# Gate products of the first two token groups: GpSimd instead of VectorE, in an attention and gated feed-forward kernel

## The chip, the cores and the metric

The kernel runs on one core of a Trainium2 chip. The metric is the device time of one execution in microseconds (us). The core has five engines that matter here: TensorE (PE, with its weight loads on a line of their own, PEld), VectorE (DVE), ScalarE (ACT), GpSimd (POOL) and SyncE (SP), whose queue issues nearly all transfers.

## The reference

An attention without softmax (two products, k transposed times v and then q times that, followed by a normalisation of each row) gives an array x of 4608 tokens by 512. The feed-forward part is what takes the time:

```
h  = x @ w_in                                    # 4608 x 2048
sp = maximum(h, 0) + log1p(exp(-abs(h)))         # softplus
g  = h * erf(sp)                                 # the gate product
out = g @ w_out                                  # 4608 x 512
```

The third line's multiplication, `h * erf(sp)`, is the operation that the change moves.

## The kernel before

**Groups and units.** Tokens are handled in groups T = 0 to 4 of 512, and the hidden width of 2048 in 16 units f of 128. The first two groups (`FIRST = 2`) run in one loop over n = 0 to 32, with T and f from `divmod(n, FC)`, `FC = 16`. The other three groups run in a second loop, over batches of four units. The change touches only the first loop, roughly 23 us to 241 us of the profile.

**One step n of the first loop.** TensorE computes the hidden unit n (line 940 in group 0; line 589 in group 1, where each operand is cut into a high and a low part and the product is collected in two PSUM tiles, `n_ps` and `m_ps`). ScalarE copies the unit to `h_sb` (lines 953 and 955), and in group 1 VectorE adds the second part, `m_ps`, from PSUM (line 567). ScalarE then computes softplus into `s_sb` (line 971). The function `erf` (line 885) turns `s_sb` into erf in place, for four units at once at the end of each batch of four; in group 1 a batch is split into two calls in neighbouring steps. Then `gates(n)` (line 881) multiplies `hs[n]` by `ss[n]` in place. Five steps after a unit was computed (`LAG = 5`), `project` (line 645) multiplies its gate product with `w_out`. In group 1, all steps share the single pair of PSUM tiles `n_ps` and `m_ps`: the products of step n + 1 into `m_ps` can begin only when VectorE's addition (line 567) of step n has read it.

**Where the gate products stand.** Each step of both groups from n = 4 on issues one, `gates(n - 4)`. In group 1 it stands after the addition of line 567. The products of the last four units, n = 28 to 31 (`whole` is 28), are issued together after the loop:

```
    for n in range(whole, FIRST * FC):
        gates(n)
    low_room.close()
    room.close()
```

After `room.close()`, the memory of the first loop, with the buffers of `h_sb` and `s_sb`, is given to new pools. The first four transfers into one of them, `w_out_parts` (line 834), are issued by SyncE next. The second loop then cuts the tile `h` of the last four units into parts on ScalarE (line 527).

**What else VectorE does in the first loop.** The program order is fixed by hand, and every engine works through its instructions in order. In group 0, VectorE rebuilds weights from loaded words (`w_join`: lines 261, 264, 267 and 274); the word buffers `w_raw` are four in number, and SyncE loads the next one (lines 224 and 229) when line 267 has read the old one. In group 1, VectorE cuts weights into parts (`w_lower`: lines 554 and 557), which line 589 uses a step later and SyncE stores, and it adds line 567. In both, it prepares the attention of the next group (lines 329, 353, 426, 440, 441, 476, 479, 488) and its parts (530 and 533). GpSimd has no work after the first 11 us.

Of the kernel before, what the change touches and what calls it, by code (L numbers as in the profile page):

```python
# [44 lines left out]
ALU = mybir.AluOpType  # L45
# [24 lines left out]
def kernel(  # L70
# [10 lines left out]
    nc = tc.nc  # L81
# [120 lines left out]
    for p in range(NP):  # L202
        nc.gpsimd.dma_start(
            out=q_last[p % 2 * R : p % 2 * R + R, p // 2],
            in_=q[0, 2 * p : 2 * p + 2, G:S, :].rearrange("h r d -> r h d"),
        )
    for i in range(2):
        nc.gpsimd.dma_start(
            out=g_col[i * D : i * D + D, :], in_=g_norm.rearrange("(d one) -> d one", one=1)
# [661 lines left out]
    hs, ss, plain = {}, {}, {}  # L871
# [6 lines left out]
        return i < len(w_order) and w_order[i][0] <= n + ahead  # L878

    def gates(n):  # L880
        nc.vector.tensor_tensor(out=hs[n], in0=hs[n], in1=ss[n], op=ALU.mult)  # L881

    def erf(units):
        for i in units:
# [2 lines left out]
    for n in range(FIRST * FC + 1):  # L887
# [27 lines left out]
        if T == 0 and done >= 0:  # L915
            gates(done)
# [30 lines left out]
        if T < FIRST:  # L947
# [9 lines left out]
            if T == FIRST - 1:  # L957
                if f == 1:
                    x_both = wide.tile([P, KC, G], FP32R, name="x_both", tag="b")
                    for i in range(0, KC, 2):  # L960
                        both_only(x_high[:, i : i + 2], x_low[:, i : i + 2], x_both[:, i : i + 2])
                    x_forms[T] = x_high, x_low, x_both
                gates(done)
                for key in list(w_new):
                    w_lower(*key)
                for key in to_cut[f]:
                    w_upper(*key)
# [26 lines left out]
    for n in range(whole, FIRST * FC):  # L994
        gates(n)
# [9 lines left out]
    def part(h, half):  # L1005
        return h[:, :, half * 2 * P : half * 2 * P + 2 * P]
# [36 lines left out]
    for m in range(first_batch, batches + 1):  # L1043
# [81 lines left out]
        for j in range(J):  # L1125
# [19 lines left out]
            for half in due_halves:  # L1145
                nc.vector.tensor_tensor(  # L1146
                    out=part(h, half), in0=part(h, half), in1=part(s, half), op=ALU.mult
# [38 lines left out]
```

## Time and profile before

| what | value |
| --- | --- |
| median of 3 runs | 907.48 us (907.44 to 908.41) |
| the profiled execution: its own time, and its span | 907.2 us, 905.4 us |
| PE busy, share of the span | 897.1 us, 99% |
| DVE busy | 758.7 us, 84% |
| ACT busy | 593.2 us, 66% |
| POOL busy | 4.7 us, 1%, in 14 instructions |
| gate products of line 881 | 32, 0.68 to 0.69 us each in the middle |

The span runs from the first to the last instruction of the profiled execution; its own time is 1.8 us more. A line such as "L881 DVE TENSOR_TENSOR" names the line of the kernel, the engine and the operation. In a timeline the columns are start, duration, engine, line, operation, output and inputs, and in square brackets the idle time before the instruction and what ended it.

### The profile page before, as it was taken

Reading aid. Unit: us, or ns where it says so; the run is one execution under the profiler, and the core shown is the slowest. Engines: PE = TensorE matmul, PEld = TensorE weight load, DVE = VectorE, ACT = ScalarE, POOL = GpSimd, SP = SyncE. Lnnn points to the kernel's source line nnn. Section 1 sums busy time; section 2 is a strip of 40 time slices with the busy share of each in tenths; the row PEclk is TensorE's granted clock in tenths of the full one; section 3 lists DMA queues with packets and bytes.
Section 4 is the critical chain, followed back from the end, with each engine's and each line's share of the span. In section 5 each row is a group of like instructions: output and inputs, shape, how many; then the busy total and the mean of one; then the engine's idle time right before and its main releaser. Section 6 shows DMA issues by size and latency. Waiting matters only on the chain.

```text
span 905.4 us, 13399 instructions
## 1 busy us (share of the span) xinstructions
PE 897.1 (99%) x4934; PEld 667.6 (74%) x4934; DVE 758.7 (84%) x1093; ACT 593.2 (66%) x784; POOL 4.7 (1%) x14
## 2 busy tenths in 40 slices
PE   8999999999999999999999999999999999999998
PEld 4444446666688888888888888888888888888886
DVE  5799959997788888888888888888888888887677
ACT  5976677775766666665666666666666766665552
POOL 2000000000000000000000000000000000000000
PEclk9999999999999999999999999999999999999999
DMA  9977308999599988988899879988797788778871
GB/s 290 300 225 222 100 30 289 367 343 354 200 377 375 328 297 262 376 306 300 300 328 364 310 238 327 362 303 305 277 346 274 266 311 311 285 285 314 320 265 48
DMA packets 136930, 259.89 MB, mean 287 GB/s; under 512 B 78817, under 2 KB 87265, under 8 KB 136865
## 3 DMA queue, kind: packets, MB, share of 16 engines
q1 hardware_dynamic: 136128, 258.09, 81.3%
q10 hardware_dynamic: 544, 0.82, 0.3%
q8 instruction: 39, 0.64, 0.3%
q14 instruction: 27, 0.21, 0.1%
q0 software_dynamic: 192, 0.13, 0.0%
HBM read 224.40 MB, written 34.60 MB: 286 GB/s over the span
## 4 chain that ended last, share of the span: by engine, by line
PE 94%; DMA 2%; DVE 2%; ACT 1%; issue 0%; SPq 0%; DVEq 0%
PE n_ps L589 48%; PE m_ps L589 24%; PE o_ps L645 10%; PE h_ps L940 5%; PE at_ps L418 2%; PE at_ps L404 2%; DMA w_out_parts<-w_out 1%; DMA w_raw<-in_moe_w_out_dram 1%; PE at_ps L456 1%; PE at_ps L457 1%; PE warm_ps L792 1%; DVE w_e L267 0%; PE o_ps L712 0%; DVE w_in_sb L274 0%; DVE h L881 0%
## 5 line engine op out<-in xcount | busy, mean ns | idle before, releaser
L589 PE MATMUL n_ps<-w_out_parts,g_forms 128*128 128x512 f32 x928 | 230.5, 390 | 0.1
L589 PE MATMUL n_ps<-x_forms,w_in_parts 128*128 128x512 f32 x896 | 224.3, 392 | 0.0
L589 PEld LDWEIGHTS n_ps<-w_out_parts,g_forms 128*128 128x128 f32 x928 | 172.7, 188 | 36.0 <-DMA w_out_parts<-w_out 0.5
L589 PEld LDWEIGHTS n_ps<-x_forms,w_in_parts 128*128 128x128 f32 x896 | 166.6, 188 | 35.6 <-ACT s_sb L885 0.2
L567 DVE TENSOR_TENSOR h<-m_ps,h 128x512 f32<-128x512 f32 x116 | 78.1, 687 | 63.9 <-PE m_ps L589 61.9
L589 PE MATMUL m_ps<-w_out_parts,g_forms 128*128 128x512 f32 (+1 forms) x468 | 124.2, 388 | 0.0
L589 PE MATMUL m_ps<-x_forms,w_in_parts 128*128 128x512 f32 x448 | 119.7, 389 | 0.0
L1092 ACT ACTIVATE h<-n_ps 128x512 f32<-128x512 f32 x112 | 66.2, 594 | 75.0 <-PE n_ps L589 74.7
L1097 ACT ACTIVATE s<-h 128x512 f32<-128x512 f32 x112 | 68.3, 629 | 70.0 <-DVE h L567 70.0
L645 PE MATMUL o_ps<-w_out_sb,h_sb 128*128 128x512 f32 x224 | 101.5, 596 | 0.2 <-DVE h_sb L881 0.2
L589 PEld LDWEIGHTS m_ps<-w_out_parts,g_forms 128*128 128x128 f32 x468 | 87.4, 188 | 18.4
L589 PEld LDWEIGHTS m_ps<-x_forms,w_in_parts 128*128 128x128 f32 x448 | 84.1, 188 | 17.5
L567 DVE TENSOR_TENSOR e<-m_ps,e 128x512 f32<-128x512 f32 (+1 forms) x117 | 80.3, 687 | 15.4 <-PE m_ps L589 5.6
L645 PEld LDWEIGHTS o_ps<-w_out_sb,h_sb 128*128 128x128 f32 x224 | 41.3, 189 | 45.3 <-issue 43.1
L533 DVE SCALAR_TENSOR_TENSOR g_forms<-g_forms 128x1024 fp32r<-128x1024 f32 x58 | 71.1, 1225 | 2.0
L530 DVE TENSOR_TENSOR g_forms<-h,g_forms 128x1024 fp32r<-128x1024 f32 x58 | 70.5, 1216 | 1.1 <-ACT g_forms L527 1.1
L527 ACT ACTIVATE g_forms<-h 128x1024 fp32r<-128x1024 f32 x58 | 58.4, 1049 | 15.3 <-DVE h L1146 7.9
L562 DVE SCALAR_TENSOR_TENSOR e<-n_ps,e 128x512 f32<-128x512 f32 x88 | 60.2, 684 | 7.3 <-PE n_ps L589 7.3
L940 PE MATMUL h_ps<-xT,w_in_sb 128*128 128x512 f32 x144 | 65.1, 595 | 1.1 <-DVE w_in_sb L274 1.1
L1146 DVE TENSOR_TENSOR h<-h,s 128x1024 f32<-128x1024 f32 x56 | 65.9, 1218 | 0.0
L116 ACT ACT_TABLE_LOAD x44 | 56.5, 1283 | 0.8
L940 PEld LDWEIGHTS h_ps<-xT,w_in_sb 128*128 128x128 f32 x144 | 26.9, 190 | 35.4 <-issue 31.4
(138 smaller groups left out, 999.0 us busy)
## 6 DMA issues: line engine op xcount, KB each, us to landing
w_out_parts<-w_out SPq DMA_DIRECT2D x116, 768.0 KB, 6.8
w_in_parts<-w_in SPq DMA_DIRECT2D x112, 768.0 KB, 6.7
w_in<-w_new SPq DMA_DIRECT2D x16, 768.0 KB, 4.6
k_sb<-in_k_dram SPq DMA_DIRECT2D x32, 288.0 KB, 6.3
v_sb<-in_v_dram SPq DMA_DIRECT2D x31, 288.0 KB, 6.3
w_raw<-in_moe_w_in_dram SPq DMA_DIRECT2D x16, 512.0 KB, 5.6
w_raw<-in_moe_w_out_dram SPq DMA_DIRECT2D x8, 1024.0 KB, 5.1
out_dram<-e SPq DMA_DIRECT2D x32, 256.0 KB, 3.5
```

Source lines behind the costliest of these rows:

```text
L116: nc.scalar.preload_act_table_set("softplus")
L527: nc.scalar.activation(high, x, AF.Copy, scale=1.0 + 2.0**-13)
L530: nc.vector.tensor_tensor(out=low, in0=x, in1=high.bitcast(FP32), op=ALU.subtract)
L533: nc.vector.scalar_tensor_tensor(out=both, in0=low.bitcast(FP32), scalar=SHIFT, in1=high.bitcast(FP32), op0=ALU.mult, op1=ALU.add,)
L562: nc.vector.scalar_tensor_tensor(out=out_, in0=ps, scalar=scale, in1=out_, op0=ALU.mult, op1=ALU.add)
L567: nc.vector.tensor_tensor(out=out_, in0=ps, in1=out_, op=ALU.add)
L589: nc.tensor.matmul(ps[:, cols], lhsT=weights(form, k), rhs=moving(form, k)[:, cols], start=(form == forms[0] and k == 0), stop=(form == fo ...
L645: nc.tensor.matmul(o_ps[j], lhsT=g[:, j * P : j * P + P], rhs=w_out_sb[:, f, :], start=(f == 0), stop=last,)
L940: nc.tensor.matmul(plain[i], lhsT=w_in_sb[:, i % FC, c], rhs=xT[T][:, c, :], start=(c == 0), stop=(c == KC - 1),)
L1092: nc.scalar.activation(h[:, i], n_ps, AF.Copy, scale=SHIFT - 1.0)
L1097: nc.scalar.activation(s[:, i], h[:, i], AF.Softplus)
L1146: nc.vector.tensor_tensor(out=part(h, half), in0=part(h, half), in1=part(s, half), op=ALU.mult)
```

## The change

`gates` issues its multiplication on GpSimd. Nothing else in the program is edited: TensorE, ScalarE and SyncE keep their instructions and order, and VectorE's list is the old one without the 32 products. The products of the second loop (line 1146) stay on VectorE.

```
     def gates(n):
-        nc.vector.tensor_tensor(out=hs[n], in0=hs[n], in1=ss[n], op=ALU.mult)
+        nc.gpsimd.tensor_tensor(out=hs[n], in0=hs[n], in1=ss[n], op=ALU.mult)
```

On GpSimd the 32 products stand one behind the other, after the work of the start. The waits of `project` (line 645), of ScalarE's copies into reused `h_sb` buffers (953 and 955), of its cut of line 527 and of SyncE's first `w_out_parts` transfer (834), which were on VectorE's products, are now on GpSimd's.

## The prediction

> **What bounds the kernel now.** I read the page's busy times first, then busy time by stage.
>
> ```profile
> PE 897.1 (99%) x4934; PEld 667.6 (74%) x4934; DVE 758.7 (84%) x1093; ACT 593.2 (66%) x784; POOL 4.7 (1%) x14
> ```
> ```profile
> 60.00:80.00 20.00, 20.00 (x95) 9.43 (x94) 18.74 (x26) 16.77 (x21) 0.00 (x0) 1.00 0.66 199
> 180.00:200.00 20.00, 20.00 (x112) 12.40 (x112) 18.62 (x33) 14.68 (x24) 0.00 (x0) 1.00 0.91 346
> ```
>
> The columns after the stretch are its length, PE, PEld, DVE, ACT, POOL busy (with counts), granted clock and DMA. TensorE is never idle in either stage, at full clock: a relieved VectorE cannot speed it up. VectorE is 93% busy, so there is little room to make it slower. The waits of TensorE between 30 and 270 us say how much there is to win, the same small sum:
>
> ```profile
> PE h_ps L940 <- DVE w_in_sb L274: 0.4, 1, 0.4
> PE o_ps L645 <- DVE h_sb L881: 0.2, 1, 0.2
> ```
> The weight loads add one of 0.5 us, for `w_out_parts`. So the change can gain about 1.1 us at most.
>
> Next, three places where VectorE is near TensorE's path. First, the timelines of ScalarE and VectorE at the first erf batch:
>
> ```profile
> 39.16 2.19 ACT L885 ACTIVATE s_sb<-s_sb 128x512 f32<-128x512 f32 x4
> ...
> 39.70 0.69 DVE L264 TENSOR_SCALAR w_e<-w_e 128x1024 int32<-128x1024 int32 x1
> 40.43 1.23 DVE L267 SCALAR_TENSOR_TENSOR w_e<-w_raw,w_e 128x1024 int32<-128x1024 int32 x1
> 41.80 1.22 DVE L274 CUSTOM_DVE_ANT_0 w_out_sb<-w_e,w_m 128x2048 uint16<-128x2048 uint16 x1
> 42.94 0.68 DVE L881 TENSOR_TENSOR h_sb<-h_sb,s_sb 128x512 f32<-128x512 f32 x1
> 45.47 0.23 DVE L426 COPY x_last<-at_ps 128x64 f32<-128x64 f32 x1 [1.85 <-ACT qT L423]
> ```
> By the chain of waits, line 267's end lets SP issue a `w_raw` load at 41.73; it lands at 46.55, VectorE joins, and TensorE resumes at 50.53, having waited. Line 267 is on the path.
>
> Second, a group 1 step (VectorE, then TensorE):
>
> ```profile
> 182.29 0.69 DVE L554 SCALAR_TENSOR_TENSOR w_new<-w_new,w_in_sb 128x512 fp32r<-128x512 f32 x1
> 183.01 0.69 DVE L557 TENSOR_TENSOR w_new<-w_new 128x512 fp32r<-128x512 f32 x1
> ...
> 184.95 0.68 DVE L567 TENSOR_TENSOR h_sb<-m_ps,h_sb 128x512 f32<-128x512 f32 x1
> ...
> 188.35 1.10 PE L589 MATMUL m_ps<-x_both,w_new 128*128 128x512 f32 x4
> ```
> The addition ends at 185.63 and must end by 188.35, when TensorE writes `m_ps` again: 2.7 us of slack. At 211.82 (next use 215.22) it is 2.7 again, elsewhere 3 to 6 (addition lines against the next `m_ps` lines).
>
> Third, the group's end, in the chain that ended last:
>
> ```profile
> 233.73 0.61 DVE h_sb L881
> ...
> 238.47 1.90 DVE h L881 x3
> ...
> 240.42 0.34 SPq L834
> ...
> 241.76 10.20 DMA w_out_parts<-w_out
> ...
> 252.01 0.73 PE n_ps L589 x2
> ```
> The last four products delay the first `w_out_parts` transfers, and TensorE waits for them at 252.
>
> **What the Trainium skill says.** "GPSIMD Engine Reference", 3.1 Elementwise: a fp32 two-input operation of 2048 elements takes 4497 ns there and 2293 on VectorE, and the input port allows about 2.6 cycles an element at 1.2 GHz. The trace has no such GpSimd instruction; its VectorE side agrees (line 1146 at half the elements: 1218 ns). "SBUF — State Buffer", Who interferes with whom: GpSimd shares a port pair with VectorE; a GpSimd operation that reads SBUF and a VectorE operation with two SBUF inputs, or in a two-port mode, exclude each other, and the later one "**fully blocks**". No run here shows it yet. "VectorE: DVE Perf Modes", The perf-mode tier table: fp32 single-input SBUF operations run at double rate. The trace agrees (0.69 us for line 264 against 1.23 for two-input line 267, both 1024 wide). So 264, 267, 274, 530, 533, 554 and 557 are in conflict; 567, 426, 353 and 678 read PSUM with at most one SBUF input and are not.
>
> **The change part by part.**
>
> Removed from VectorE: 32 x 0.60 us (start to start, 42.94 to the next; 0.68 with the overlapped end) = 19 us. TensorE is full beside it; what this gives is room for what follows.
>
> Price of one product on GpSimd: scaling 4497 by 512/2048 gives 1.12 us as lower bound; a fixed 0.3 us (the upper end that I allow) gives (4497-300)/4 + 300 = 1.35. I take 1.2, an estimate from that page. Alone it is hidden: the products no longer wait in VectorE's queue, so they start when erf ends. The first is ready at 39.8 and `project` wants it at 45.68 by TensorE's line; later ones have more. The extra waits on TensorE, ScalarE and SP replace equal ones on VectorE, so I cost them at nothing, covered by that earliness; with no earliness the first `project` has 2.1 us (43.62 to 45.68). GpSimd's own waits for buffer reuse are for work steps earlier; nothing else queues on it.
>
> (A) First batch, +1.2 us. Product 0 is ready while 264 runs; I take the port to go alternately to whoever waited longest. So product 0 goes in front of 267, which is 1.2 late, as are the `w_raw` load and its join, and TensorE's wait at 50.53 grows from 0.4 to 1.6. 274 becomes 2.4 late and ends at 45.4, just before `project` at 45.68. The 1.85 us idle time then takes the rest. Bounds: 0 (GpSimd loses the port) and 2.4 (two products in front). Later batches of group 0: nothing, since the joins are 6 us or more ahead of use (73.69 against 80.05), and VectorE idles 3.6 us at 119 and 6.3 at 129.
>
> (B) Group 1, +1.8 us. Erf comes in pairs, two pairs in neighbouring steps, so four products fall in some 5 us (erf at 153.8 and 157.0; 181.1 and 184.7; 208.0 and 211.1). Cluster one: four blocks less two removed products are 4.8 - 1.2 = 3.6, against 3.7 (the weight part ends 163.26, line 589 takes it at 166.93) and 4.0 at `m_ps`; nothing. Cluster two: three products run before the addition, 3 x 1.2 - 0.6 = 3.0 against 2.7: +0.3. What is left is 4.8 - 0.6 - 0.3; VectorE's idle times to 208 give back 0.9, four removed products 2.4, so 0.6 remains. Cluster three: 3.6 + 0.6 - 2.7 = +1.5. Bounds: 0 if the port is not contended; if each block also costs VectorE a second 1.2 (a turn lost on either side), A is 2.4 and B (7.2 - 0.6 - 2.7) + (7.2 - 2.7) = 8.4. After 220 VectorE idles 3.5 us twice (lines 567 and 476), and all lateness there ends.
>
> (C) Group end, +0.8 us. The four erfs end 235.71 + 0.63 and then every 0.52 to 237.90. On VectorE the products waited behind a copy (678) and ended 240.36. On GpSimd the first starts at about 236.35, and four end at 236.35 + 4.8 = 241.15. No conflicting VectorE operation runs then. SP's four loads move by 0.8, and TensorE's wait for them grows by that. ScalarE's line 527 moves too; its next on the path, 423 at 244.90, waited 1.5 us anyway, and VectorE's 0.4, 0.2 and 1.3 us idle behind it take the rest. The 0.2 us that `project` gains at 234.38 vanishes in the same wait. Bounds: -0.5 (the whole wait gone) and +1.4 (at 1.35 each).
>
> Sum 1.2 + 1.8 + 0.8 = +3.8 us on 907.2 is 911.0. The median stands 0.3 above that execution: 911.3. Afterwards TensorE is busy to the end, so nothing gives it back.
>
> **The rivals.** What a measurement of this kernel can tell from no change is about 0.2%, 1.8 us.
>
> *Not slower: the port does not matter.* VectorE's instructions follow with overlapping ends (0.60 apart at 0.68 long), so GpSimd may find it only in gaps and PSUM operations, or share it freely. Place: line 267 at 40.43. If that starts before 40.8, A and B are near zero and C remains: 908.3. For it: VectorE's gaps suffice for the due times; against it: the skill's exclusive lock.
>
> *Much slower.* Under contention a product costs VectorE 2.4 us: A 2.4, B 8.4, C 0.8: +11.6 on 907.5, 919. For it: VectorE's 93% load; against it: light windows after 115 and 220.
>
> *Faster.* VectorE's relief removes TensorE's waits: 907.5 - 1.1 = 906.4. Only if a product takes under 1 us and never blocks.
>
> **How the numbers follow.** Forecast 0.53, port harmless 0.29, much slower 0.15, faster 0.03. Forecast and much slower lie above +1.8 us, but for 0.02 of the forecast's low side: slower 0.66. Harmless, that 0.02 and most of the faster case stay within: same 0.33, faster 0.01. The range runs from 907.4, C at its low end, to 917.5; beyond lie most of the faster case and most of the much slower one, about 0.15.
>
> **What would show it.** In the changed profile: POOL with 32 more instructions of about 1.2 us (over 1.5 beside VectorE's two-input ones); VectorE's line 267 near 41.6 and TensorE's wait at line 940 near 1.6; gaps in front of 530, 533, 554 and 557 right where POOL runs; new TensorE waits on 567 or 557 near 188 and 215; SP's first `w_out_parts` near 241.2 plus the earlier delay. Wrong it is if VectorE's lines keep their places, or if the wait for `w_out_parts` does not grow.

## The result: 0.3% slower, by three stalls of TensorE

| | before | after |
| --- | --- | --- |
| median | 907.42 us (906.76 to 908.41, 8 runs) | 910.12 us (909.35 to 910.77, 8 runs) |
| profiled execution, own time | 907.2 us | 909.53 us |
| its span | 905.4 us | 907.4 us |

The ratio is 1.003, with a 95% interval of 1.0021 to 1.0038: 2.7 us slower by the medians, against 3.8 us predicted. The two profiled executions differ by 2.3 us in time and by 2.0 us in span.

The page of the changed kernel, busy time of each engine, and the two groups of the moved products among the instructions of line 881 (minimum, median and maximum in ns, then first and last start in us):

```profile
PE 896.9 (99%) x4934; PEld 667.3 (74%) x4934; DVE 758.8 (84%) x1061; ACT 593.1 (65%) x784; POOL 54.4 (6%) x46
```
```profile
L881 POOL TENSOR_TENSOR h_sb<-h_sb,s_sb x28: 1264/1707/2262, 39.6 to 215.4; 128x512 f32<-128x512 f32 x28
L881 POOL TENSOR_TENSOR h<-h,s_sb x4: 1273/1286/1290, 238.0 to 241.7; 128x512 f32<-128x512 f32 x4
```

VectorE lost 32 instructions and is busy for just as long: 758.8 us against 758.7. The relief of some 19 us was spent by its other instructions, which now take longer. On GpSimd, the four products at the end, beside which VectorE has at most one copy out of PSUM, take 1.27 to 1.29 us; the median of the other 28 is 1.71. What TensorE waited for between 30 and 275 us (total, times, longest):

```profile
PE n_ps L589 <- DMA w_out_parts<-w_out: 1.1, 1, 1.1
PE m_ps L589 <- DVE h_sb L567: 1.0, 1, 1.0
PE h_ps L940 <- DVE w_in_sb L274: 0.9, 1, 0.9
```

All three places of the prediction are there, and the wait for the gate product near 234 is gone. TensorE's 4934 instructions have one order in both kernels, so the start of the k-th in one trace can be set against the k-th in the other. That difference is -0.27 us after the first 10 us (it varies there from run to run, before any product). It drifts by -0.10 in small steps near 145 us, as it does in runs where nothing was moved before that time. Apart from this it changes only at these places:

| TensorE's instruction, time before | change of the difference, us |
| --- | --- |
| 50.5, line 940, after the join | +0.54 |
| 188.4, line 589, first into `m_ps` | +1.22 |
| 215.5, line 589, into `m_ps` | +0.11 |
| 234.4, line 645, project of unit 27 | -0.51 |
| 252.0, line 589, first `w_out_parts` | +1.04 |

The sum, 2.40 less 0.27 and 0.10, is the span's 2.0 us. After 252 us nothing changes: TensorE is busy to the end.

The three places in the changed kernel's trace. First, VectorE's timeline at the first erf batch:

```profile
40.16 2.18 DVE L267 SCALAR_TENSOR_TENSOR w_e<-w_raw,w_e 128x1024 int32<-128x1024 int32 x1
42.48 2.09 DVE L274 CUSTOM_DVE_ANT_0 w_out_sb<-w_e,w_m 128x2048 uint16<-128x2048 uint16 x1
45.21 0.22 DVE L426 COPY x_last<-at_ps 128x64 f32<-128x64 f32 x1 [0.64 <-ACT qT L423]
...
46.28 1.21 DVE L261 TENSOR_SCALAR w_e<-w_raw 128x1024 f32<-128x1024 f32 x1
```

Lines 267 and 274 take 2.18 and 2.09 us where they took 1.23 and 1.22. The added time lies inside their durations, not in idle time before them. Line 426 waited 1.85 us for ScalarE before and now waits 0.64, so that delay is absorbed. Line 261 takes 1.21 instead of 0.68. In the kernel before, that line and the end of its join were:

```profile
46.54 0.68 DVE L261 TENSOR_SCALAR w_e<-w_raw 128x1024 f32<-128x1024 f32 x1
...
49.25 1.22 DVE L274 CUSTOM_DVE_ANT_0 w_in_sb<-w_e,w_m 128x2048 uint16<-128x2048 uint16 x1
```

Second, VectorE in the group 1 step, lines 530 and 533 in the kernel before, and the chain of waits in the changed one:

```profile
183.22 0.68 DVE L554 SCALAR_TENSOR_TENSOR w_new<-w_new,w_in_sb 128x512 fp32r<-128x512 f32 x1
183.94 1.65 DVE L557 TENSOR_TENSOR w_new<-w_new 128x512 fp32r<-128x512 f32 x1
185.51 1.76 DVE L530 TENSOR_TENSOR x_forms<-x,x_forms 128x512 fp32r<-128x512 f32 x1
187.31 1.67 DVE L533 SCALAR_TENSOR_TENSOR x_forms<-x_forms 128x512 fp32r<-128x512 f32 x1
188.90 0.68 DVE L567 TENSOR_TENSOR h_sb<-m_ps,h_sb 128x512 f32<-128x512 f32 x1
```
```profile
183.62 0.68 DVE L530 TENSOR_TENSOR x_forms<-x,x_forms 128x512 fp32r<-128x512 f32 x1
184.34 0.69 DVE L533 SCALAR_TENSOR_TENSOR x_forms<-x_forms 128x512 fp32r<-128x512 f32 x1
```
```profile
188.90 0.69 DVE h_sb L567
...
189.63 1.20 PE m_ps L589 x4
```

Lines 557, 530 and 533 have two inputs from SBUF and take about 1 us longer. Line 567 has one from PSUM and keeps its 0.68. The chain goes from its end straight to TensorE's write of `m_ps`.

Third, the chain at the group's end:

```profile
241.78 1.25 POOL h L881
...
243.05 0.34 SPq L834
...
244.39 9.59 DMA w_out_parts<-w_out
...
254.03 0.73 PE n_ps L589 x2
```

GpSimd's last product releases the transfers, and TensorE waits for them.

### The profile page after: what moved, and what is told of

It is laid out like the page before. It is cut to its first block, busy times and chain, and to the rows that moved or that the text cites. A ratio compares the mean times of both kernels' runs of the same rounds, so it can differ in the third digit from the quotient of the medians.

```text
span 907.4 us, 13464 instructions
## 1 busy us (share of the span) xinstructions
PE 896.9 (99%) x4934; PEld 667.3 (74%) x4934; DVE 758.8 (84%) x1061; ACT 593.1 (65%) x784; POOL 54.4 (6%) x46
## 4 chain that ended last, share of the span: by engine, by line
PE 87%; issue 4%; DVE 3%; DMA 3%; ACT 2%; POOL 0%; POOLq 0%; SPq 0%; DVEq 0%; ACTq 0%
PE n_ps L589 46%; PE m_ps L589 23%; PE o_ps L645 6%; PE h_ps L940 5%; PE at_ps L418 2%; PE at_ps L404 2%; DMA w_out_parts<-w_out 1%; DMA w_in<-w_new 1%; PE at_ps L456 1%; PE at_ps L457 1%; DMA w_raw<-in_moe_w_out_dram 1%; PE warm_ps L792 1%; ACT w_new L551 0%; DVE w_e L267 0%; DVE w_new L557 0%
## 5 line engine op out<-in xcount | busy, mean ns | idle before, releaser
L881 POOL TENSOR_TENSOR h_sb<-h_sb,s_sb 128x512 f32<-128x512 f32 x28 | 44.7, 1620 | 161.6 <-ACT s_sb L885 119.2
```

## Experiments

All differ from the kernel before in `gates` alone. Where only some products are moved, the edit is

```
-        nc.vector.tensor_tensor(out=hs[n], in0=hs[n], in1=ss[n], op=ALU.mult)
+        side = nc.gpsimd if CONDITION else nc.vector
+        side.tensor_tensor(out=hs[n], in0=hs[n], in1=ss[n], op=ALU.mult)
```

so that the lines after it move down by one. Times are medians; "shift" is the change of TensorE's difference against the kernel before, as in the table above.

### The group's end alone: `n >= 28`

> Only the products n = 28 to 31 are on GpSimd. Theory (the group's end is its own cost): they run one by one at about 1.27 us from the end of the first erf, SP's first w_out_parts transfer is about 0.8 to 0.9 us later against the end of the erfs, TensorE's wait for w_out_parts grows from 0.5 to about 1.4 us, and TensorE is 0.9 us late from there to the end: +0.9 us. No earlier shift. Rival (the late start of w_out_parts came from the earlier lateness of VectorE, not from GpSimd's slower products): 0, at most 0.2 us.

Measured: 908.36 us against 907.38, ratio 1.0011 (1.0004 to 1.0017): +1.0 us. One shift, +0.8, at 252. TensorE's wait there and the chain of waits:

```profile
PE n_ps L589 <- DMA w_out_parts<-w_out: 0.9, 1, 0.9
```
```profile
240.79 1.25 POOL h L882
...
242.06 0.34 SPq L834
...
253.31 0.73 PE n_ps L589 x2
```

The rival falls: four products one behind the other cost about 1 us by themselves (by the times; 0.8 in the profiled execution).

### All but the group's end: `n < 28`

> Only the products n = 0 to 27 are on GpSimd; the last four stay on VectorE. Theory (shared port plus group end add up): TensorE is late by 0.5 us at the join near 50, by another 1.0 near 189 and 0.2 near 216, and wins back 0.2 to 0.4 at the last project: about +1.3 us at the end. Rival (all of the loss comes from the group's end): below +0.3 us.

Measured: 908.87 us against 907.38, ratio 1.0014 (1.0008 to 1.0021): +1.5 us. Shifts of +0.5 near 50, +1.0 at 188, +0.2 in small steps from there to 223, -0.5 at 234 and -0.1 at 252. Both parts are real, and together (1.0 + 1.5) they give what the full change gives (2.7) within the intervals.

### The first batch: `n < 4` and `n < 3`

> Only the products n = 0 to 3 are on GpSimd. Both theories expect TensorE's wait at line 940 near 50.5 us to grow by about 0.5 us, +0.5 us in all: VectorE's lines 267 and 274 take about 2.2 us instead of 1.2, as they did with all 32 moved.

> Only the products n = 0 to 2 are on GpSimd; product 3 is back in VectorE's queue, behind the join of line 274. Theory Q (VectorE's own queue carries the delay: lines 267 and 274 are late, but VectorE's idle time before line 426 takes that up, and only product 3, beside line 261, delays the join that TensorE waits for): TensorE's shift near 50.5 us falls to 0 to 0.1 us. Theory L, as predicted (line 267's end lets SP issue a w_raw load, and that load sets the join): lines 267 and the load stay late by 0.7 to 1 us, and TensorE's shift stays 0.5 us or more.

With four products, TensorE's wait at line 940 is 0.9 us (shift +0.5); with three, it is 0.4 as before (no shift). The times, 907.58 and 907.49 us against 907.38, cannot tell these apart (1.0002, 0.9994 to 1.0011, and 1.0004, 0.9996 to 1.0012); the profiles can. VectorE and SyncE with three products:

```profile
40.95 2.18 DVE L267 SCALAR_TENSOR_TENSOR w_e<-w_raw,w_e 128x1024 int32<-128x1024 int32 x1
43.27 2.09 DVE L274 CUSTOM_DVE_ANT_0 w_out_sb<-w_e,w_m 128x2048 uint16<-128x2048 uint16 x1
46.00 0.22 DVE L426 COPY x_last<-at_ps 128x64 f32<-128x64 f32 x1 [0.64 <-ACT qT L423]
...
47.07 0.69 DVE L261 TENSOR_SCALAR w_e<-w_raw 128x1024 f32<-128x1024 f32 x1
```
```profile
43.20 0.37 SPq L229 DMA_DIRECT2D w_raw<-in_moe_w_out_dram  x1
```

and VectorE's line 261 with four:

```profile
47.06 1.20 DVE L261 TENSOR_SCALAR w_e<-w_raw 128x1024 f32<-128x1024 f32 x1
```

Lines 267 and 274 are equally stretched in both, and the `w_raw` load is issued equally late (43.20 and 43.18). Only line 261 differs, by 0.5 us, and so does TensorE. Theory Q holds and theory L, the prediction's, falls: the late load leaves TensorE where it was, and what costs is product 3 beside line 261, after VectorE's idle time has been used up.

### The second cluster of group 1, alone and after the first: `20 <= n < 24` and `16 <= n < 24`

> Only the four products n = 20 to 23, the second cluster of the second group, are on GpSimd. Theory (lateness carried over from the first cluster by way of a w_new store made the second one cost 1.0 us): with nothing carried in, VectorE's addition of line 567 near 185 ends within its 2.7 us of slack or misses it by no more than 0.4, so TensorE loses 0 to 0.4 us near 188. Rival (the second cluster costs its 1.0 us by itself, through three contended VectorE instructions): 0.8 to 1.2 us.

> The products n = 16 to 23, first and second cluster of the second group, are on GpSimd. Theory (carry): as with all moved, ScalarE's line 551 waits near 171 for a store of w_new, VectorE's addition near 178 is about 1.2 us later than in the kernel before, and TensorE loses about 1.0 us near 188. Rival (no carry): the same loss as with the second cluster alone.

The second cluster alone: 908.94 us against 907.41, ratio 1.0018 (1.001 to 1.0026): +1.5 us, shift +1.6 at 188. VectorE's timeline:

```profile
182.35 1.78 DVE L554 SCALAR_TENSOR_TENSOR w_new<-w_new,w_in_sb 128x512 fp32r<-128x512 f32 x1
184.17 1.65 DVE L557 TENSOR_TENSOR w_new<-w_new 128x512 fp32r<-128x512 f32 x1
185.74 1.75 DVE L530 TENSOR_TENSOR x_forms<-x,x_forms 128x512 fp32r<-128x512 f32 x1
187.53 1.67 DVE L533 SCALAR_TENSOR_TENSOR x_forms<-x_forms 128x512 fp32r<-128x512 f32 x1
189.12 0.68 DVE L567 TENSOR_TENSOR h_sb<-m_ps,h_sb 128x512 f32<-128x512 f32 x1
```

My expectation failed: with nothing carried in, the cluster costs more, not less. All four products come before the addition, four stretches sum to 4.1 us, and 4.1 less the 2.7 of slack is 1.4. The rival's mechanism is right, its size (three stretches) too small. In the full change VectorE comes later to this place, only three products fall ahead of the addition, and the loss is smaller, 1.2.

Both clusters: 909.47 us against 907.41, ratio 1.0023 (1.0013 to 1.0032): +2.1 us, and TensorE waits 2.2 us at `m_ps`. (The profiled execution, the slowest of its nine at 911.58 us, had a lower granted TensorE clock for some 4 us after that wait, 0.5 from 192 to 194 us, so nothing after 190 us is read from it.) ScalarE's timeline shows how lateness travels:

```profile
171.97 0.63 ACT L551 ACTIVATE w_new<-w_out_sb 128x512 fp32r<-128x512 f32 x1 [1.29 <-DMA w_out<-w_new]
173.82 0.63 ACT L551 ACTIVATE w_new<-w_in_sb 128x512 fp32r<-128x512 f32 x1 [1.23 <-DMA w_in<-w_new]
```

VectorE finishes its weight parts late, SyncE stores them late, and ScalarE waits to write the same `w_new` buffer again. Its later work, down to the input of line 476, is late with it. The addition of line 567 that comes just ahead of the cluster (178.47 before, 181.79 here) is 2.6 us late after taking off the 0.68 by which this run was late from its start. So the carry exists, and adds to what the cluster costs by itself: TensorE's wait is 2.2 us here and 1.3 with the second cluster alone. The medians, with overlapping intervals, don't separate the two runs. Both numbers are about twice what I expected (1.2 late, 1.0 lost). Here ScalarE waited for two stores, 2.5 us in all; in the changed kernel it waits for one, 1.2 us.

### Is it the port? Products stay, GpSimd reads or only writes

Here every product stays on VectorE, and GpSimd touches the used-up tile:

```
         nc.vector.tensor_tensor(out=hs[n], in0=hs[n], in1=ss[n], op=ALU.mult)
+        if 16 <= n < 24:
+            nc.gpsimd.tensor_tensor(out=ss[n], in0=ss[n], in1=ss[n], op=ALU.mult)
```
```
+        if 16 <= n < 24:
+            nc.gpsimd.memset(ss[n], 0.0)
```

> All products stay on VectorE as before. After each of the products n = 16 to 23, GpSimd squares the used-up s_sb tile in place (two inputs from SBUF, nobody reads the result). No work waits on GpSimd but the reuse of that buffer two units later. Port theory: VectorE's two-input instructions beside it (lines 554, 557, 530, 533) take about 1.65 us instead of 0.69, as they did with the products moved, and the additions of line 567 stay at 0.68; these eight come one a step, not in clusters, so TensorE loses 0 to 0.5 us. Rival (VectorE was slow because of waits on the moved products): all at 0.69, no loss.

> As in the run with the dead squares, but GpSimd fills the used-up s_sb tile with zeros instead: it writes SBUF and reads none. Theory (the shared thing is the read side of the port): VectorE's instructions keep 0.68 to 0.69 us beside it, no loss. Rival (the whole port is shared): the same stretch beside it, of some 0.3 to 0.6 us each.

One of the eight places in each run, first with the reading GpSimd, then with the writing one (GpSimd's lines move down by two):

```profile
188.17 0.68 DVE L554 SCALAR_TENSOR_TENSOR w_new<-w_new,w_out_sb 128x512 fp32r<-128x512 f32 x1
188.39 1.36 POOL L883 TENSOR_TENSOR s_sb<-s_sb 128x512 f32<-128x512 f32 x1 [5.88 <-DVE h_sb L881]
188.89 1.41 DVE L557 TENSOR_TENSOR w_new<-w_new 128x512 fp32r<-128x512 f32 x1
```
```profile
186.05 0.69 DVE L554 SCALAR_TENSOR_TENSOR w_new<-w_new,w_out_sb 128x512 fp32r<-128x512 f32 x1
186.25 0.53 POOL L883 MEMSET s_sb<- 128x512 f32 x1 [5.99 <-DVE h_sb L881]
186.77 0.69 DVE L557 TENSOR_TENSOR w_new<-w_new 128x512 fp32r<-128x512 f32 x1
```

Work that nobody waits for makes VectorE's line 557 beside it 0.72 us longer when it reads SBUF; this is so at seven of the eight places, and no engine waits for the squares in that profile. When it only writes, VectorE's lines keep their lengths. There the line to look at is 554, also with two inputs from SBUF: the fill runs almost wholly beside it at seven of the eight places and ends as 557 starts. Line 554 keeps its 0.68 to 0.69 us, and the fill takes its 0.53 us there as at the eighth place, where hardly anything stands beside it: neither holds up the other. The first kernel takes 908.93 us against 907.28 (1.0018, 1.0011 to 1.0025), with shifts that sum to about +1.3 between 196 and 223, more than the 0.5 that I had allowed; the second 907.52 (1.0001, 0.9993 to 1.001). So such a loss needs no wait on moved products. The stretch is smaller than 0.96 because less of the reading instruction was left when line 557 came: 0.86 us (188.89 to the square's end at 189.75), against 1.10 with the moved product at line 557 in the changed kernel (183.94 to 185.04).

### Versions that might beat both: `n in (27, 28)`, and seventeen products

> Only products 27 and 28 are on GpSimd, as a version that may beat both. Product 27 no longer stands behind line 567 in VectorE's queue, so the last project starts 0.2 us earlier; product 28 runs on GpSimd from the end of its erf, so VectorE has three products left and ends them 0.6 us earlier, and w_out_parts starts 0.6 us earlier. TensorE's waits there (0.2 and 0.5 us) go: -0.5 to -0.7 us against before. Rival (GpSimd and VectorE exclude each other on the port, product 29 waits for product 28 and the gain is lost): 0 to -0.2 us.

> Seventeen of the 32 products are on GpSimd, those for which the runs so far showed no loss or a gain: n = 0 to 2, 4 to 15, 27 and 28. Product 3, the pairs of the second group's clusters and 29 to 31 stay on VectorE. Theory (only three places cost): no TensorE loss near 50, 188 and 216, the gain of 0.2 to 0.5 us near 234 and of 0.3 to 0.5 at w_out_parts, -0.4 to -0.7 us against before. Rival (fifteen products in the first group cost by lateness that is carried on, such as through w_raw loads): 0 or slower.

The condition of the second is `n < 3 or 4 <= n < 16 or n in (27, 28)`. Measured: 907.04 us against 907.41 (0.9993, 0.9985 to 1.0001), and 906.95 against 907.28 (0.9996, 0.9987 to 1.0004). In both profiles, between 30 and 275 us, TensorE has one wait left, the join's:

```profile
PE h_ps L941 <- DVE w_in_sb L274: 0.4, 1, 0.4
```

The waits near 234 and 252 are gone, as expected. The shifts there are -0.5 and -0.4 in both versions. Only the one at 234 can be put down to the edit: at 252 the run with the writing GpSimd wins 0.4 too, with no edit near. The medians point to a gain of 0.3 to 0.4 us, less than expected, and neither interval excludes none. In the second profile TensorE's difference does not change from 23 to 234 us, so the fifteen products moved in the first group cost it nothing there.

## Why the prediction was right, and where its steps were off

**The port decides: right.** The forecast rested on the port shared by GpSimd and VectorE, an exclusive lock as the Trainium skill has it ("SBUF — State Buffer", Who interferes with whom). The runs agree on the instructions in conflict, line 261 apart (see A), and on GpSimd's reads, not its writes, being what meets a two-input VectorE instruction. Turns taken alternately were an assumption of mine; with the second cluster alone, four products stretch four VectorE instructions in a row (182.35 to 187.53), one each. The rival in which the port does not matter is out: 267 stretches at 40.16 and two-input lines do at 184. But the sign that I named for telling the two apart was wrong. I looked for a later start of line 267 (near 41.6, and before 40.8 if the port is harmless) and for gaps in front of the blocked lines. Line 267 starts at 40.16 and there are no gaps, since the delay lies inside the durations; read by the starts, the wrong case would have been chosen.

**The price of a product: 1.2 us taken, 1.27 measured** alone, and 1.22 to 1.25 from start to start in a row. What it costs a VectorE instruction is less than that: 1.65 - 0.69 or 2.18 - 1.23, about 0.96, up to 1.09.

**(A) +1.2 predicted, +0.5 measured, and the path was another.** Product 0 did go in front of line 267. But the chain's link from the `w_raw` load to line 261 was none: in the changed kernel 261 starts at 46.28, 3.9 us after that load's issue at 42.41, while the shortest landing of such a load between 28 and 60 us of the kernel before takes 4.1. In the kernel before, the landing at 46.55 and line 261's start at 46.54 fell together by chance. The load is of `w_out` words, and the join that follows ends in `w_in_sb` (line 274 at 49.25), so it could not have waited for it. The step that failed is taking an inferred link for a wait without asking what VectorE was doing just before. It was just ending line 354. The line that did cost, 261, is missing from the prediction's list of lines in conflict, though it is of the kind of line 264, which is in it.

**(B) +1.8 predicted, +1.3 measured (+0.3 and +1.5 predicted, +1.2 and +0.1 measured).** The mechanism, the addition of line 567 missing `m_ps`, held. The terms did not. At cluster two I called cluster one harmless and let VectorE come without lateness. In fact it was 1.36 late (line 567 at 180.00 against 178.47, less the 0.17 of TensorE's own difference at that time). ScalarE and VectorE in the changed kernel, then line 567 in the kernel before:

```profile
172.03 0.63 ACT L551 ACTIVATE w_new<-w_in_sb 128x512 fp32r<-128x512 f32 x1 [1.19 <-DMA w_in<-w_new]
...
177.06 0.69 DVE L476 SCALAR_TENSOR_TENSOR u<-at_ps,u 128x512 f32<-128x512 f32 x1 [0.30 <-ACT u L470]
...
180.00 0.65 DVE L567 TENSOR_TENSOR h_sb<-m_ps,h_sb 128x512 f32<-128x512 f32 x1
```
```profile
178.47 0.65 DVE L567 TENSOR_TENSOR h_sb<-m_ps,h_sb 128x512 f32<-128x512 f32 x1
```

The account is 1.36 - 0.6 for the removed product + 3.0 for three stretches = 3.8, against 2.7 of slack: 1.1, and 1.2 was measured. The missing term was the reuse of `w_new`, through its store and ScalarE. At cluster three, lateness before the removed product was 0.26 (206.99 against 205.34, less 1.39). Less 0.6 and plus 3.0 that is 2.7, just the slack, and the stall is 0.1. My 1.5 came from stretches of 1.2 and a lateness left over that was not there.

**(C) +0.8 predicted, +1.0 in the full change; alone, +0.8 in the profile and +1.0 by time.** Four products one by one, SyncE's transfers, TensorE: each step as predicted. The prediction let the small gain at 234 vanish in the wait at 252. The gain was 0.5, not 0.2, and the net of both places is +0.5.

**The sum** was 3.8; the medians say 2.7, and the steps of the two profiles 2.4. The over-sized A and cluster three outweigh the under-sized cluster two. That errors of opposite sign met in one sum is luck: the direction was earned by the mechanism, the closeness of the total was not. The low end of the range doesn't follow from its reason either: (C) at -0.5 with the other parts at zero is 907.0, not 907.4. No later batch of the first group moved TensorE, as predicted.

**Open.** TensorE's difference after the first 10 us varied between -0.3 and +0.9 us among these runs, and in several the stretch at 252 gave 0.3 to 0.4 us back without any edit near it (0.3 with three and with four products, 0.4 with the writing GpSimd). Why was not tried. It bears on every shift given at 252, which is to be read with that much doubt.

## What to carry to other kernels

An engine with idle time is no free place for work if it shares a port with the engine that is relieved: count what each moved instruction does to the neighbours that run beside it, and look when it becomes ready, since products that come in bursts pile their stretches up in front of one due time. Slack should be summed up to each due time, with the lateness that buffers and their stores carry around. A link in the chain of waits is an inference: before a step rests on it, see whether the engine itself was busy until then.

## What was not expected of the hardware

A GpSimd product of 128x512 fp32 takes 1.27 us alone; beside VectorE's two-input instructions both get longer, the product to between 1.5 and 2.3 us, and most of VectorE's 0.69 us instructions to 1.65 to 1.78. The exclusion itself costs VectorE less than the product's whole length, 0.96 against 1.27. A GpSimd fill of 128x512 that only writes took 0.53 us and left VectorE's two-input 0.69 us instruction beside it untouched.
